# A cosformer attention feeding a leaky-ReLU feed-forward: the first batch's k tails are loaded and prepared first, and its preparation work is dealt out differently between ScalarE and VectorE

## The chip, the cores and the metric

The kernel runs on one core of one Trainium2 chip. The metric is the device time of one execution in microseconds, as the median of several runs. The kernel before takes 294.44 us (three runs, 294.29 to 294.61).

A core has five engines that work through their own instruction queues and meet by semaphores: TensorE (PE in the profile, with its weight loads as PEld), VectorE (DVE), ScalarE (ACT), GpSimd (POOL) and SyncE (SP), which here issues nearly all of the DMA transfers. Main memory is HBM, on-chip memory is SBUF, and the matmul accumulators are in PSUM.

## The reference

Eight batches, eight heads, 576 positions, 64 elements a head. Each of q and k is cut at zero and weighted by the cosine and by the sine of its position, so that a head has 128 features; then a linear attention is formed, and its output is fed to a two-layer network with a leaky ReLU.

```python
def phi(x, c, s):
    r = np.maximum(x, 0.0)
    return np.concatenate([r * c, r * s], axis=-1)
q_p = phi(q, cos_w, sin_w)
k_p = phi(k, cos_w, sin_w)
kv = np.einsum('bhsf,bhsd->bhfd', k_p, v)
z = np.sum(k_p, axis=2)
num = np.einsum('bhsf,bhfd->bhsd', q_p, kv)
den = np.einsum('bhsf,bhf->bhs', q_p, z)[..., None] + 1e-06
attn = num / den
...
x = attn.transpose(0, 2, 1, 3).reshape(B * S, H * D)   # 4608 x 512
h = x @ w_in                                          # 512 x 2048
out = np.maximum(0.01 * h, h) @ w_out                 # 2048 x 512
```

## The kernel before

The 4608 rows go through the network in nine groups of 512: the 512 "main" positions of each of the eight batches, and a ninth group made of the eight 64-position "tails". Weights are cast to float16 once and stay in SBUF. From about 19 us on TensorE runs the two layers back to back, and the attention of the next batch is woven between them. The change lies wholly in what comes before that: the attention of batch 0, which no network work can cover, because the network has nothing to work on yet.

There is no scheduler. The order of the text is the order of every engine's queue, and an engine that waits holds up everything behind it in its own queue.

How batch 0 goes, with the names of the code:

- SyncE issues the loads in the order of the text. `load_main` fetches half of the heads (0 to 3, or 4 to 7) of q, k or v into a staging buffer, 512 KB in rows of 1 KB. `load_kvtail` fetches the 64 tail positions of k or v as two transfers of 64 KB in rows of 256 bytes. Before, the order is q half 0, q half 1, k tail, k half 0, v tail, v half 0, k half 1, v half 1, and then w_in. All of these go through one queue; there are seven staging buffers.
- `idle(n)` issues n matmuls on a tile of zeros, whose result nobody reads. They keep TensorE running while it has nothing to do.
- `q_prep` makes the float16 features of q: for each of two head halves and each j of four position groups one cosine and one sine instruction (`phi_half`, line 226 on VectorE, line 224 on ScalarE). j = 3 is ScalarE's, the others VectorE's.
- `q_transpose` (line 363) turns the features of one j over on TensorE, eight heads, and copies the result from PSUM to SBUF (`qpT`; j = 0, 1, 2 on ScalarE, line 232, j = 3 on VectorE, line 234).
- `k_tail` and `k_main` make the features of k (`kpt` and `kpm`), `v_tail` and `v_main` cast v. Heads 0 to 3 come first. Their features of k are VectorE's, but for the cosine of j = 0, which is ScalarE's; their v is cast half on VectorE and half on ScalarE. For heads 4 to 7 ScalarE has all four cosines and VectorE all four sines.
- `kv_half(0, 0)` sums k features times v over the positions for heads 0 to 3 (lines 264 and 274) into PSUM (`ps_kvh`), and ScalarE copies the sum to `kv` (line 315). `kv_half(0, 1)` does the same for heads 4 to 7.
- `num_half(0, jp, hg)` multiplies q features by `kv` for two of the four j and for four heads (line 409), and `divide` divides by the denominator on VectorE in three instructions (lines 384, 388, 389), giving `xs`.
- `x_transpose_half` (line 425) turns `xs` over on TensorE, and ScalarE copies it to `xT` (line 429), which is what the first layer, `ffn1` (line 452), multiplies.
- GpSimd casts v's tail, the last quarter of v and the pieces of w_in (line 234).

For heads 0 to 3 the order of TensorE's queue after the first `kv_half` is: both `num_half`, six idle matmuls, the turning over of the first two j, `kv_half(0, 1)`, the turning over of the other two j, then the first matmuls of `ffn1` with the same steps for heads 4 to 7 between them.

Two PSUM pools matter here: "o" has two buffers, which idle matmuls, `ps_kvh` and the turned-over `xs` (`ps_xth`) take in turn; "n" has one, and "h" two.

Of the kernel before, what the change touches and what calls it, by code (L numbers as in the profile page):

```python
# [9 lines left out]
dt = mybir.dt  # L10
# [3 lines left out]
P = 128  # L14
J = 4
# [3 lines left out]
def kernel(  # L19
# [14 lines left out]
    nc = tc.nc  # L34
# [11 lines left out]
    NE = D + 2  # L46
# [25 lines left out]
    def psum(where, shape, dtype, name):  # L72
        p = {"h": ps_h, "o": ps_o, "n": ps_n}[where]
        return p.tile(shape, dtype, name=name, tag="ps_" + where)

    st = {}
    ACT, DVE, POOL = nc.scalar, nc.vector, nc.gpsimd
# [3 lines left out]
    def load_main(nm, src, b, parts=(0, 1)):  # L81

        if parts[0] == 0:
            st[nm, b] = stage.tile([P, H, J, D], dt.float32, name=f"{nm}st", tag="stage")
        lo, hi = 4 * parts[0], 4 * parts[-1] + 4
        nc.sync.dma_start(  # L86
            st[nm, b][:, lo:hi],
            src[b, lo:hi, 0:MAIN, :].rearrange("h (p j) d -> p h j d", j=J),
        )

    def load_kvtail(nm, src, b):

        t = kvtail.tile([P, H // 2, D], dt.float32, name=f"{nm}tl", tag="kvtail")
        v4 = src[b, :, MAIN:S, :].rearrange("(c o) p d -> o p c d", o=2)
        for o in range(2):
            nc.sync.dma_start(t[o * TAIL : (o + 1) * TAIL], v4[o])  # L96
        st[nm + "t", b] = t
# [20 lines left out]
    for i in range(DFF // 512):  # L118
        for c in range(0, NKC, 2):
            n = 1 if i == 0 and c == 0 else 2  # L120
# [18 lines left out]
    def load_w2(i, lo=0, hi=4):  # L139
        if lo == 0:  # L140
            st["w2", i] = stage.tile([P, 4, DM], dt.float32, name="w2st", tag="stage")
        nc.sync.dma_start(st["w2", i][:, lo:hi], w2v[i, :, lo:hi])

    load_main("q", q, 0, (0,))
    load_main("q", q, 0, (1,))
    load_kvtail("k", k, 0)
    load_main("k", k, 0, (0,))
    load_kvtail("v", v, 0)
    load_main("v", v, 0, (0,))
# [13 lines left out]
    def idle(n):  # L163
        ps = psum("o", [P, MAIN], dt.float32, "ps_idle")
        for _ in range(n):
            nc.tensor.matmul(ps, lhsT=blank[:, 0:P], rhs=blank)  # L166
# [51 lines left out]
    kv = [const.tile([P, H, NE], dt.float16, name=f"kv{b}") for b in range(B)]  # L218
# [3 lines left out]
    def phi_half(eng, o, i, col):  # L222
        if eng is ACT:
            nc.scalar.activation(o, i, AF.Relu, scale=col)
        else:
            eng.tensor_scalar(  # L226
                out=o, in0=i, scalar1=0.0, scalar2=col, op0=ALU.max, op1=ALU.mult
            )

    def copy(eng, o, i):  # L230
        if eng is ACT:
            nc.scalar.copy(o, i)  # L232
        else:
            eng.tensor_copy(o, i)  # L234

    def kp_tiles(b):
        st["kpm", b] = kppool.tile([P, H, J, F], dt.float16, name="kpm")
        st["kpt", b] = kppool.tile([P, H // 2, F], dt.float16, name="kpt")

    def k_main(b, j, eng_c, eng_s, lo=0, hi=H):  # L240
        kpm, kst = st["kpm", b], st["k", b]
        for eng, t, f in ((eng_c, cos_t, 0), (eng_s, sin_t, D)):
            phi_half(
                eng, kpm[:, lo:hi, j, f : f + D], kst[:, lo:hi, j, :], t[:, j : j + 1]
            )

    def k_tail(b, eng_c, eng_s):
        kpt, kt, c = st["kpt", b], st["kt", b], J
        phi_half(eng_c, kpt[:, :, 0:D], kt, cos_t[:, c : c + 1])
        phi_half(eng_s, kpt[:, :, D:F], kt, sin_t[:, c : c + 1])  # L250

    def v_main(b, lo, hi, eng):
        copy(eng, vmain[b % 2][:, lo:hi, :, 0:D], st["v", b][:, lo:hi])

    def v_tail(b, eng):
        for o in range(2):
            sl = slice(o * TAIL, (o + 1) * TAIL)
            copy(eng, vtail[b % 2][sl, :, o, 0:D], st["vt", b][sl])

    def kv_mm(b, hg, ps):  # L260
        kpm, kpt = st["kpm", b], st["kpt", b]
        for cc in range(2):
            c = 2 * hg + cc
            nc.tensor.matmul(
                ps[:, 2 * cc * NE : 2 * (cc + 1) * NE],
                lhsT=kpt[:, c, :],
                rhs=vtail[b % 2][:, c].rearrange("p a e -> p (a e)"),
                start=True,
                stop=False,
            )  # L270
            for o in range(2):
                h = 2 * c + o
                for j in range(J):
                    nc.tensor.matmul(  # L274
                        ps[:, (2 * cc + o) * NE : (2 * cc + o + 1) * NE],
                        lhsT=kpm[:, h, j, :],
                        rhs=vmain[b % 2][:, h, j, :],
                        start=False,
                        stop=(o == 1 and j == J - 1),
                    )  # L280
# [24 lines left out]
                )  # L305
        nc.scalar.copy(kv[b].rearrange("p (c o) e -> p o c e", o=2), ps)

    def kv_half(b, hg, where, out=True):
        st["kvh", hg] = psum(where, [P, 4 * NE], dt.float32, "ps_kvh")
        kv_mm(b, hg, st["kvh", hg])  # L310
        if out:
            kv_half_out(b, hg)

    def kv_half_out(b, hg):
        nc.scalar.copy(
            kv[b][:, 4 * hg : 4 * hg + 4].rearrange("p h e -> p (h e)"), st["kvh", hg]
        )

    def q_src(g, j):
        if g < B:  # L320
# [3 lines left out]
    def q_prep(g, j, lo=0, hi=H, eng=DVE):  # L324
        src, c, _ = q_src(g, j)
        if lo == 0 and j % 2 == 0:
            st["qp2", g, j // 2] = qppool.tile([P, 2, H, F], dt.float16, name="qp")
            for o in range(2):
                st["qp", g, j + o] = st["qp2", g, j // 2][:, o]
        qp = st["qp", g, j]  # L330
        phi_half(eng, qp[:, lo:hi, 0:D], src[:, lo:hi], cos_t[:, c : c + 1])
        phi_half(eng, qp[:, lo:hi, D:F], src[:, lo:hi], sin_t[:, c : c + 1])
# [26 lines left out]
    def q_transpose(g, j, eng, where="h"):  # L359
        qp = st["qp", g, j]  # L360
        ps = psum(where, [P, H, P], dt.float16, "ps_qt")
        for h in range(H):
            nc.tensor.transpose(ps[:, h, :], qp[:, h, :], ident)  # L363
        if j % 2 == 0:
            qpT_pair(g, j // 2)
        copy(eng, st["qpT", g, j], ps)
# [15 lines left out]
    def divide(ps, xs):  # L382
        den = small.tile([P, H], dt.float32, name="den")
        nc.vector.tensor_scalar_add(  # L384
            den.rearrange("p (a b) -> p a b", a=2), ps[:, :, D : 4 * NE : NE], 1e-6
        )
        rden = small.tile([P, H], dt.float32, name="rden")
        nc.vector.reciprocal(rden, den)  # L388
        nc.vector.tensor_tensor(  # L389
            out=xs,  # L390
            in0=ps[:, :, 0 : 4 * NE].rearrange("p a (b e) -> p a b e", e=NE)[
                :, :, :, 0:D
            ],
            in1=rden.rearrange("p (a b) -> p a b", a=2)[:, :, :, None].broadcast_to(
                [P, 2, 4, D]
            ),
            op=ALU.mult,
        )

    def num_half(g, jp, hg, where, ps=None):  # L400

        if hg == 0 and jp == 0:
            st["xs", g] = xspool.tile([P, J, H, D], dt.float16, name="xs")
        if ps is None:
            ps = psum(where, [P, 2, 512], dt.float32, "ps_numh")
        for o in range(2):
            for hh in range(4):
                h = 4 * hg + hh
                nc.tensor.matmul(  # L409
                    ps[:, o, hh * NE : (hh + 1) * NE],  # L410
                    lhsT=st["qpT", g, 2 * jp + o][:, h, :],
                    rhs=kv[g][:, h, :],
                )
        divide(ps, st["xs", g][:, 2 * jp : 2 * jp + 2, 4 * hg : 4 * hg + 4, :])
# [110 lines left out]

    for hg in range(2):
        for j in range(J):
            q_prep(0, j, 4 * hg, 4 * hg + 4, ACT if j == 3 else DVE)  # L530
    kp_tiles(0)
    q_transpose(0, 0, ACT)
    idle(1)
    q_transpose(0, 1, ACT)
    idle(1)
    k_tail(0, DVE, DVE)
    v_tail(0, POOL)
    k_main(0, 0, ACT, DVE, 0, 4)
    for j in range(1, J):
        k_main(0, j, DVE, DVE, 0, 4)  # L540
    v_main(0, 0, 2, DVE)
    v_main(0, 2, 4, ACT)
    q_transpose(0, 2, ACT, "n")
    idle(1)
    q_transpose(0, 3, DVE)
    idle(7)
    kv_half(0, 0, "o")
    for j in range(J):
        k_main(0, j, ACT, DVE, 4, 8)
    num_half(0, 0, 0, "h")  # L550
    num_half(0, 1, 0, "n")
    v_main(0, 4, 6, ACT)
    v_main(0, 6, 8, POOL)
    idle(6)
    x_transpose_half(0, 0, 0)
    kv_half(0, 1, "o")
    for part in w1_parts:
        cast_w1(*part, POOL)
    x_transpose_half(0, 1, 0)
    half = 2 * P  # L560
    ps = psum("h", [P, 2, 512], dt.float32, "ps_numh")
# [76 lines left out]
    ps = psum("n", [P, 2, DM], dt.float32, "ps_o")  # L638
# [24 lines left out]
    ps = psum("h", [P, 2, MAIN], dt.float16, "ps_x")  # L663
# [124 lines left out]
```

## Time and profile before

| | |
|---|---|
| median of three runs | 294.44 us |
| the profiled execution: time | 293.82 us |
| the profiled execution: span from the first to the last instruction | 292.0 us |
| granted TensorE clock, mean | 1.000 |
| TensorE busy | 286.4 us (98%) |
| VectorE busy | 128.7 us (44%) |
| ScalarE busy | 118.4 us (41%) |
| GpSimd busy | 12.7 us (4%) |
| chain that ended last: TensorE's share | 94% |

The profile's page says "TensorE is the bound" with one look. Idle matmuls count as busy there, though, and 30 of them are 9.9 us. What can be moved at all is the stretch before the network starts, and for that one reads the chain of waits and the order of time of each engine in the first 20 us. Times in those views are from the start of the span; each row gives start, duration, engine, line of the code, operation and tiles, and, in brackets, how long the engine had been idle before it and what ended that.

### The profile page before, as it was taken

What the parts mean: (1) busy time and instruction counts of PE and PEld (TensorE: products, weight loads), DVE (VectorE), ACT (ScalarE), POOL (GpSimd) and SP (SyncE); (2) the same over time, 40 slices, a digit from 0 to 9 for tenths busy, and PEclk for the clock granted to TensorE, in tenths of its full rate; (3) what the DMA queues carried; (4) which work ended last, traced back from release to release, by engine and by line L of the source; (5) the groups of instructions that cost most, each with busy time, mean ns of one, the idle gap of its engine ahead of it and who ended that gap; (6) DMA issues with size and microseconds to landing.
All of it is one profiled execution on the core that took longest, in us unless ns stands there. A gap on an engine that the chain in (4) does not pass through costs nothing.

```text
span 292.0 us, 4774 instructions
## 1 busy us (share of the span) xinstructions
PE 286.4 (98%) x1958; PEld 152.7 (52%) x1958; DVE 128.7 (44%) x328; ACT 118.4 (41%) x148; POOL 12.7 (4%) x24
## 2 busy tenths in 40 slices
PE   8999999999999999999999999999999999999995
PEld 3585556555555555455545554555445444444444
DVE  6931687926835816823562356333323310000011
ACT  6865266753544632632263226322222222222200
POOL 2264000000000000000000000000000000000000
PEclk9999999999999999999999999999999999999999
DMA  7999999999999999789584989504691051011133
GB/s 233 348 386 407 325 364 335 315 204 324 212 241 318 229 291 298 166 162 338 164 182 84 296 233 199 91 37 110 160 199 38 36 108 38 36 54 54 39 71 73
DMA packets 87909, 56.93 MB, mean 195 GB/s; under 512 B 55888, under 2 KB 80720, under 8 KB 87504
## 3 DMA queue, kind: packets, MB, share of 16 engines
q1 hardware_dynamic: 87808, 56.57, 71.0%
q8 instruction: 15, 0.25, 0.4%
q10 hardware_dynamic: 80, 0.07, 0.1%
q14 instruction: 6, 0.05, 0.1%
HBM read 36.70 MB, written 9.44 MB: 158 GB/s over the span
## 4 chain that ended last, share of the span: by engine, by line
PE 94%; DMA 2%; SPq 1%; ACT 1%; DVE 1%; issue 0%
PE ps_h L452 43%; PE ps_o L475 41%; PE ps_num L373 3%; PE ps_kv L299 2%; DMA vst<-in_v_dram 2%; PE ps_l L504 1%; SPq L96 1%; PE ps_xth L425 1%; PE ps_qt L363 1%; PE ps_numh L409 1%; SPq L86 1%; PE ps_kv L290 0%; PE ps_idle L166 0%; PE ps_kvh L274 0%; ACT qpT L232 0%; PE ps_xt L438 0%
## 5 line engine op out<-in xcount | busy, mean ns | idle before, releaser
L452 PE MATMUL ps_h<-xT,w 128*128 128x512 f16 (+1 forms) x592 | 142.8, 373 | 0.1
L475 PE MATMUL ps_o<-w,g 128*128 128x512 f16 x560 | 139.5, 379 | 0.0
L460 ACT ACTIVATE g<-ps_h 128x1024 f16<-128x1024 f32 x72 | 73.2, 1023 | 128.8 <-PE ps_h L452 128.8
L452 PEld LDWEIGHTS <-w 128*128 128x128 f16 x592 | 64.4, 114 | 52.3 <-issue 0.2
L475 PEld LDWEIGHTS <-g 128*128 128x128 f16 x560 | 54.2, 98 | 61.4
L234 DVE COPY osb<-ps_o 128x512 f32<-128x512 f32 x31 | 21.4, 690 | 77.1 <-PE ps_o L475 75.3
L384 DVE TENSOR_SCALAR den<-ps_num 128x8 f32<-128x8 f32 x28 | 4.6, 165 | 54.9 <-PE ps_num L373 54.9
L389 DVE TENSOR_TENSOR xs<-ps_num,rden 128x512 f16<-128x512 f32 x28 | 19.4, 691 | 1.2 <-DVE rden L388 0.2
L226 DVE TENSOR_SCALAR kpm<-kst,sin_t 128x512 f16<-128x512 f32 (+1 forms) x40 | 16.6, 429 | 1.1 <-DMA kst<-in_k_dram 1.1
L226 DVE TENSOR_SCALAR qp<-qst,cos_t 128x512 f16<-128x512 f32 (+1 forms) x34 | 15.5, 456 | 2.8 <-DMA qst<-in_q_dram 2.8
L226 DVE TENSOR_SCALAR qp<-qst,sin_t 128x512 f16<-128x512 f32 (+1 forms) x34 | 15.5, 456 | 0.0
L373 PEld LDWEIGHTS <-qpT 128*128 128x128 f16 (+1 forms) x256 | 10.6, 101 | 7.3 <-issue 1.7
L232 ACT CAST vmain<-vst 128x1024 f16<-128x1024 f32 (+1 forms) x14 | 12.5, 920 | 2.4 <-DMA vst<-in_v_dram 2.3
L226 DVE TENSOR_SCALAR kpm<-kst,cos_t 128x512 f16<-128x512 f32 (+1 forms) x29 | 13.1, 453 | 0.3 <-DMA kst<-in_k_dram 0.3
L373 PE MATMUL ps_num<-kv,qpT 128*128 128x66 f16 (+1 forms) x256 | 11.8, 194 | 0.0
L166 PE MATMUL ps_idle<-blank 128*128 128x512 f16 x30 | 9.9, 478 | 1.2 <-DVE blank L161 1.2
L234 DVE CAST w<-w2st 128x1024 f16<-128x1024 f32 (+1 forms) x6 | 5.1, 868 | 11.8 <-DMA w2st<-in_moe_w_out_dram 11.8
L232 ACT COPY qpT<-ps_qt 128x1024 f16<-128x1024 f16 x7 | 7.0, 1012 | 5.7 <-PE ps_qt L363 5.7
L234 POOL CAST w<-w1st 128x1024 f16<-128x1024 f32 (+1 forms) x9 | 8.5, 945 | 3.6 <-DMA w1st<-in_moe_w_in_dram 3.6
L388 DVE RECIPROCAL rden<-den 128x8 f32<-128x8 f32 x36 | 7.3, 203 | 1.2
L299 PE MATMUL ps_kv<-vmain,kpm 128*128 128x66 f16 x192 | 7.1, 193 | 0.0
L299 PEld LDWEIGHTS <-kpm 128*128 128x128 f16 x192 | 6.4, 98 | 0.3
(62 smaller groups left out, 99.7 us busy)
## 6 DMA issues: line engine op xcount, KB each, us to landing
out_dram<-osb SPq DMA_DIRECT2D x32, 256.0 KB, 2.5
qst<-in_q_dram SPq DMA_DIRECT2D x7, 1024.0 KB, 6.8
kst<-in_k_dram SPq DMA_DIRECT2D x6, 1024.0 KB, 9.7
vst<-in_v_dram SPq DMA_DIRECT2D x6, 1024.0 KB, 9.4
w1st<-in_moe_w_in_dram SPq DMA_DIRECT2D x7, 512.0 KB, 10.4
w2st<-in_moe_w_out_dram SPq DMA_DIRECT2D x3, 1024.0 KB, 12.9
kst<-in_k_dram SPq DMA_DIRECT2D x4, 512.0 KB, 6.9
vst<-in_v_dram SPq DMA_DIRECT2D x4, 512.0 KB, 7.9
```

The costliest lines, as they stand in the source:

```text
L166: nc.tensor.matmul(ps, lhsT=blank[:, 0:P], rhs=blank)
L226: eng.tensor_scalar(out=o, in0=i, scalar1=0.0, scalar2=col, op0=ALU.max, op1=ALU.mult)
L232: nc.scalar.copy(o, i)
L234: eng.tensor_copy(o, i)
L299: nc.tensor.matmul(ps[:, h % 2, h // 2], lhsT=kpm[:, h, j, :], rhs=vmain[b % 2][:, h, j, :], start=False, stop=(h >= H - 2 and j == J - 1),)
L373: nc.tensor.matmul(ps[lo:hi, h // 4, (h % 4) * NE : (h % 4 + 1) * NE], lhsT=qpT[:, h, lo:hi], rhs=kv[b][:, h, :],)
L384: nc.vector.tensor_scalar_add(den.rearrange("p (a b) -> p a b", a=2), ps[:, :, D : 4 * NE : NE], 1e-6)
L388: nc.vector.reciprocal(rden, den)
L389: nc.vector.tensor_tensor(out=xs, in0=ps[:, :, 0 : 4 * NE].rearrange("p a (b e) -> p a b e", e=NE)[:, :, :, 0:D], in1=rden.rearrange("p (a ...
L452: nc.tensor.matmul(ps[:, m % 2, lo:hi], lhsT=w1[m // 4, c][0][:, w1[m // 4, c][1], m % 4 : 512 : 4], rhs=xT[:, lo // P : hi // P, c, :], s ...
L460: nc.scalar.activation(st["g", g][:, m - 1 : m + 1, :], ps, AF.Lrelu)
L475: nc.tensor.matmul(st["ps_o", g, tt], lhsT=st["g", g][:, m, tt * P : (tt + 1) * P], rhs=w2[:, m, :], start=(m == 0), stop=(m == NFT - 1),)
```

## The change

Five edits, all for batch 0:

1. The k tail's two loads go ahead of both halves of q; `k_tail` goes ahead of all of `q_prep` on VectorE.
2. The cosine of j = 1 of k, heads 0 to 3, moves from VectorE to ScalarE.
3. The copy of the first `kv` (heads 0 to 3) moves from ScalarE to VectorE; `kv_half` takes the engine as an argument (and loses an unused option).
4. For heads 4 to 7 the features of k for j = 0 and 1 come first, then the multiplication and division for j = 0 and 1 of heads 0 to 3, then the features for j = 2 and 3, then the second multiplication and division. Before, all four j of k came ahead of both.
5. Three idle matmuls instead of six ahead of the first turning over of `xs`.

```diff
+    load_kvtail("k", k, 0)
     load_main("q", q, 0, (0,))
     load_main("q", q, 0, (1,))
-    load_kvtail("k", k, 0)
     load_main("k", k, 0, (0,))
...
-    def kv_half(b, hg, where, out=True):
-        st["kvh", hg] = psum(where, [P, 4 * NE], dt.float32, "ps_kvh")
-        kv_mm(b, hg, st["kvh", hg])
-        if out:
-            kv_half_out(b, hg)
...
+    def kv_half(b, hg, where, eng=ACT):
+        ps = psum(where, [P, 4 * NE], dt.float32, "ps_kvh")
+        kv_mm(b, hg, ps)
+        copy(eng, kv[b][:, 4 * hg : 4 * hg + 4].rearrange("p h e -> p (h e)"), ps)
...
+    kp_tiles(0)
+    k_tail(0, DVE, DVE)
     for hg in range(2):
         for j in range(J):
             q_prep(0, j, 4 * hg, 4 * hg + 4, ACT if j == 3 else DVE)
-    kp_tiles(0)
     q_transpose(0, 0, ACT)
     idle(1)
     q_transpose(0, 1, ACT)
     idle(1)
-    k_tail(0, DVE, DVE)
     v_tail(0, POOL)
-    k_main(0, 0, ACT, DVE, 0, 4)
-    for j in range(1, J):
-        k_main(0, j, DVE, DVE, 0, 4)
+    for j in range(J):
+        k_main(0, j, ACT if j < 2 else DVE, DVE, 0, 4)
     v_main(0, 0, 2, DVE)
     v_main(0, 2, 4, ACT)
...
-    kv_half(0, 0, "o")
-    for j in range(J):
-        k_main(0, j, ACT, DVE, 4, 8)
-    num_half(0, 0, 0, "h")
-    num_half(0, 1, 0, "n")
+    kv_half(0, 0, "o", DVE)
+    for jp in range(2):
+        for j in range(2 * jp, 2 * jp + 2):
+            k_main(0, j, ACT, DVE, 4, 8)
+        num_half(0, jp, 0, "n" if jp else "h")
     v_main(0, 4, 6, ACT)
     v_main(0, 6, 8, POOL)
-    idle(6)
+    idle(3)
     x_transpose_half(0, 0, 0)
     kv_half(0, 1, "o")
```

More of the change, by code (lines that the diff above doesn't have):

```diff
@@ L306, in kv_all @@
         nc.scalar.copy(kv[b].rearrange("p (c o) e -> p o c e", o=2), ps)
-    def kv_half(b, hg, where, out=True):
-        st["kvh", hg] = psum(where, [P, 4 * NE], dt.float32, "ps_kvh")
-        kv_mm(b, hg, st["kvh", hg])
-        if out:
-            kv_half_out(b, hg)
[L314 to L317, printed above, removed]
+    def kv_half(b, hg, where, eng=ACT):
+        ps = psum(where, [P, 4 * NE], dt.float32, "ps_kvh")
+        kv_mm(b, hg, ps)
+        copy(eng, kv[b][:, 4 * hg : 4 * hg + 4].rearrange("p h e -> p (h e)"), ps)
     def q_src(g, j):
```

## The prediction

> **What bounds the kernel now.** I read the chain of waits first. In time order it shows what held the start up:
>
> ```profile
> 5.19 5.22 DMA vst<-in_v_dram
> 10.43 0.62 ACT vmain L232
> 11.05 0.91 ACT qpT L232
> 11.96 0.29 ACT kv L315
> 12.29 0.67 PE ps_numh L409 x16
> 12.96 1.29 PE ps_idle L166 x6
> 14.61 0.59 ACT xT L429
> 15.24 0.38 PE ps_xth L425 x4
> 18.82 12.11 PE ps_h L452 x64
> ```
>
> From 18.82 us on the chain is TensorE without a hole. Ahead of that it hangs on the landing of v's first half (10.41), then on ScalarE, where the copy of `kv` stands behind a copy of `qpT`. The point to follow is 15.24: the second turning over of `xs` (j = 2, 3). Whatever it shifts by, `ffn1` and all later work of TensorE shift by.
>
> Then the timeline of SyncE's queue, VectorE and ScalarE in the same stretch:
>
> ```profile
> 0.73 1.01 SPq L86 DMA_DIRECT2D qst<-in_q_dram  x2
> 1.79 1.40 SPq L96 DMA_DIRECT2D ktl<-in_k_dram  x2
> 3.23 0.60 SPq L86 DMA_DIRECT2D kst<-in_k_dram  x1
> ...
> 4.65 0.35 DVE L226 TENSOR_SCALAR qp<-qst,cos_t 128x256 f16<-128x256 f32 x1 [1.20 <-DMA qst<-in_q_dram]
> 6.29 0.51 ACT L224 ACTIVATE qp<-qst,cos_t 128x256 f16<-128x256 f32 x1 [0.54 <-DMA qst<-in_q_dram]
> 11.94 1.14 DVE L226 TENSOR_SCALAR kpm<-kst,sin_t 128x256 f16<-128x256 f32 x4 [0.29 <-DMA kst<-in_k_dram]
> 14.46 0.69 DVE L389 TENSOR_TENSOR xs<-ps_numh,rden 128x512 f16<-128x512 f32 x1
> ```
>
> q's halves are waited for at 4.65 and 6.29, k's second half at 11.94. From 11.94 VectorE does four sines and two divisions without a hole until 14.46 + 0.69 = 15.15: 3.21 us. That chain, from a landing, ends 0.09 us ahead of 15.24.
>
> The table of windows shows when the transfers start (the last two columns are the DMA engines' busy share and GB/s):
>
> ```profile
> 1.75:2.00 0.25, 0.25 (x2) 0.00 (x0) 0.25 (x1) 0.25 (x1) 0.25 (x1) 1.00 0.13 37
> 2.75:3.00 0.25, 0.25 (x2) 0.13 (x1) 0.23 (x2) 0.24 (x2) 0.03 (x1) 1.00 1.06 365
> ```
>
> First bytes about 1.1 us after the first issue, then a ramp of 0.9 us to a full share. In windows of 3 us the share stays between 1.01 and 1.21 from 3 to 63 us: the transfers are one saturated stream, so a delay at its head is a delay of every landing up to there.
>
> Last, the next place where TensorE meets a landing, batch 1's first turning over of `xs`:
>
> ```profile
> 44.77 1.14 DVE L226 TENSOR_SCALAR kpm<-kst,sin_t 128x256 f16<-128x256 f32 x4 [0.82 <-DMA kst<-in_k_dram]
> 47.29 0.69 DVE L389 TENSOR_TENSOR xs<-ps_numh,rden 128x512 f16<-128x512 f32 x1
> 48.09 0.61 PE L425 MATMUL ps_x<-ident,xs 128*128 128x128 f16 x8
> ```
>
> `xs` is done at 47.98 from a landing at 44.77, and read at 48.09. So a start that is earlier by more than about 0.1 us is taken back here, unless the stream is earlier too; a later stream has the same 0.1 us.
>
> **The change part by part.**
>
> *The k tail ahead of q in the queue.* Its two issues take 1.40 us from 1.79, so q's first issue moves from 0.73 to about 2.1, by 1.36 (1.40 less the 0.04 between issues that stands there either way). k's half stays at 3.23, and all behind it. How much later q lands is bounded from both sides. Below: from q's second half (6.26) to the v tail (issued 4.53, landing 4.4 later, 8.93) the stream carried two tails and 512 KB; the next 512 KB halves came 1.5 apart (10.41, 11.94), so a 128 KB tail costs (2.67 - 1.53) / 2 = 0.57, about 0.5 with the reading error of the landings. But q's first packet cannot come before its issue: 2.1 + 1.1 = 3.2, where the stream before had already moved 0.32 MB of q by the quarter-microsecond windows. At 380 GB/s, the rate after the ramp, that is 0.85; so q is 0.85 late at the least. Above: the ramp, an engine by engine start, is paid again, and q is late by the whole 1.36. I take 1.15, nearer to the upper end, since the ramp's row is one in which issue and not bandwidth decides. Everything behind q no longer has the tail ahead of it in the stream, which gives 0.5 back: late by 0.65 (ends 0.35 and 0.86).
>
> A rule of the Trainium skill speaks to the size of that 0.5: "DMA: Bandwidth & Descriptors", section "Why small descriptors are slow (HBM only)", charges pieces of 256 bytes 27% on top. By it the tail takes 128 KB / 380 GB/s x 1.27 = 0.44, and the stream would be 0.71 late, not 0.65; the row decides.
>
> *VectorE ahead of `kv`.* The tail's two sines and cosines (2 x 0.265 by their start-to-start) go into the wait for q, and one cosine leaves. They are a new wait at the head of VectorE's queue, with all of `q_prep` behind it; the second tail issue ends near 2.1, 3.7 ahead of q's landing, and the shortest issue to landing at that time is 3.8 for 512 KB, so I count it as covered (a tail that lands after 5.3 would delay q's features one for one). With q at 5.80 and 7.44: six instructions to 7.39, six to 9.03, then six for k (before eight with the tail's) from k's landing 8.43 + 0.65 = 9.08 to 10.67. v lands at 10.41 + 0.65 = 11.06, so VectorE waits for it: cast 11.08 to 11.50, `qpT` of j = 3 (0.68) to 12.15. The 0.8 us taken off VectorE is spent waiting.
>
> *ScalarE ahead of `kv`.* The first copy of `qpT` needs the first j of q's second half, so it moves by 1.15, from 7.39 to 8.54. Two copies take 1.82 (7.39 to 9.21): 10.36. Two cosines instead of one, 0.41 each: 11.18. Before, ScalarE then had 0.71 of idle time until v landed; now the delay and the moved cosine use it up. v's cast goes 11.18 to 11.80 (before 10.43 to 11.05), and behind it `qpT` of j = 2 (0.91). The matmuls of heads 2, 3 need that cast: 11.85 to 12.27 (before 11.41 to 11.83), +0.44.
>
> *The copy of `kv` on VectorE.* No row has it there. Bounds: 0.29, what the chain gives ScalarE for it, and 0.45 (a division's 128x8 costs 0.15, 512 elements out of PSUM 0.69, so 264 come to 0.43). I take 0.40. On ScalarE it would have waited for `qpT` until 12.7, so here the move is right: 12.30 to 12.70, and the multiplication starts at 12.74 (before 12.29). Behind it on VectorE stand the four sines; k's second half lands at 11.94 + 0.65 = 12.59, so they lose 0.11 to the copy.
>
> *The divisions.* Their order changes, not their sum: two sines to 13.23, the division for j = 0, 1 (its matmuls done at 13.08) to 14.3, two sines, the second division. The first `xs` is done at 14.3, not 14.11, and the last at 12.70 + 3.21 = 15.91; the second turning over follows at 15.96 against 15.24: **+0.72**. Even with every landing where it was, this chain could not end before 11.94 + 3.21 = 15.15.
>
> *Heads 4 to 7.* ScalarE is free of `qpT` at 12.62, four cosines (1.61) to 14.23, v (landed 14.1) to 14.83; `kv_half(0, 1)` then runs 14.89 to 15.6, ahead of 15.96. It costs nothing under that cover; without it 0.4 would show.
>
> *Three idle matmuls fewer.* 0.65 us of TensorE that waited for `xs` anyhow: nothing. The PSUM buffer that the second turning over takes is freed by ScalarE's `xT`, 0.94 after the first turning over begins (14.26 to 15.20): 14.35 + 0.94 = 15.3, ahead of 15.96. GpSimd's v cast and the casts of w_in move with the stream, 0.65; w_in's third piece is done at 17.2 and first used at 18.65, so that slack stays.
>
> *At 48 us* the stream is 0.65 late with 0.1 of slack, TensorE 0.72: no further wait.
>
> **The sum:** 293.82 + 0.72 = 294.54 for an execution like the profiled one. That one is 0.62 below the median of the runs, so on the median 295.16; I say **295.15**.
>
> **The rivals.** *No second ramp* (q 0.85 late, stream 0.35). ScalarE: 7.39 + 0.85 + 1.82 + 0.82 = 10.88, v to 11.50, matmuls 11.55 to 11.97, `kv` to 12.4, then 3.21: 15.61, turning over at 15.66, +0.42: **294.85**. For it: the engines are already running when q's issue reaches them; against: each of the 16 DMA engines gets its part of q only after the issue.
>
> *Not slower: the tails travel in the ramp.* If they fill the 0.9 us in which the engines stand half empty, and issue faster as the first in the queue, the stream behind them is earlier by some 0.1: k at 11.84, `kv` already copied, xs at 15.05, -0.1: **294.3**. It decides only if two tails are issued in less than about 0.9 us; the shortest of 32 tail issues took 0.607, so two take 1.2. A larger gain meets the wait at 48 us. Both bounds hold whatever the moved cosine and copy save.
>
> *TensorE's clock falls.* With q late, TensorE turns over heads 0 to 3 of j = 0 by 6.9, and waits till 8.05. The first 512-column matmuls take 427 ns each, later ones 216, so it starts at half speed. If the gap of 1.1 us sends it back until about 13, `kv_half` (0.72 from 11.10 to 11.83) doubles, and the first eight matmuls of the multiplication (0.25) do: some 0.95 on top of the forecast, **296.1**. Against: the gap from 11.83 to 12.29, short as it is, did nothing. "TensorE: Matmul & The Clock Gate" of the Trainium skill, "What's actually happening", has the clock fall after an idle window of about 3.4 us. By it this gap is too short, but part 4 of that page adds that transposes do not count as work; the trace shows no fall either way.
>
> **How the numbers follow.** Forecast 54% (own range 294.95 to 295.4), no second ramp 24%, not slower 12%, clock 10%. The range 294.3 to 295.9 takes in the first three and leaves out the clock and a little on either side. A measurement of this kernel can tell 0.2%, 0.59 us, from no change. Slower by more: the forecast but for its lower part, and the clock, 58%. Within: no second ramp, most of "not slower", that lower part, 37%. Faster 5%.
>
> **What would show it.** Right: q's first wait on VectorE ends near 5.8 and its second at 7.4, k's second half lands near 12.6, the second turning over near 16.0; an idle VectorE ahead of v's cast. Wrong: q's first wait ends before 5.2, or k's second half by 12.0; a `kv` copy over 0.5; 512-column matmuls of 427 ns after 8 us. A new wait of TensorE after 19 us would break the sum too.

## The result, and the profile after

| | before | after |
|---|---|---|
| median | 294.26 us (6 runs, 293.89 to 294.61) | 296.35 us (6 runs, 295.75 to 297.88) |
| ratio, with its 95% interval | | 1.0074 (1.0050 to 1.0098) |
| profiled execution: time, span | 293.82, 292.0 us | 296.38, 294.6 us |

The change costs 2.1 us. It was forecast to cost 0.7, with 295.9 as the far end of the range.

The chain of waits of the kernel after, with start, duration and what ran:

```profile
2.21 4.59 DMA qst<-in_q_dram
6.82 2.20 DVE qp L226 x8
9.07 0.40 PE ps_qt L357 x4
...
11.46 1.51 PE ps_idle L166 x7
...
13.63 0.43 DVE kv L234
14.06 0.53 DVE kpm L226 x2
...
15.00 0.69 DVE xs L383
15.69 0.99 DVE kpm L226 x2
...
17.03 0.70 DVE xs L383
17.78 0.40 PE ps_xth L419 x4
...
21.37 12.11 PE ps_h L446 x64
```

The chain no longer begins with v's landing but with q's. From there it goes through the features of q, their turning over, `kv`, then sines and divisions in turn, to the second turning over of `xs`. That one stood at 15.24 and is now at 17.78: +2.54, and the span is longer by 2.6. Two equal sounding rows differ: the sines at 14.06 took 0.53 for two, those at 15.69 took 0.99.

The timeline of the kernel after, in brackets the idle time before the row and what ended it:

```profile
0.73 1.44 SPq L96 DMA_DIRECT2D ktl<-in_k_dram  x2
2.21 1.16 SPq L86 DMA_DIRECT2D qst<-in_q_dram  x2
...
6.82 0.35 DVE L226 TENSOR_SCALAR qp<-qst,cos_t 128x256 f16<-128x256 f32 x1 [2.13 <-DMA qst<-in_q_dram]
8.21 0.51 ACT L224 ACTIVATE qp<-qst,cos_t 128x256 f16<-128x256 f32 x1 [0.42 <-DMA qst<-in_q_dram]
12.21 0.43 DVE L234 CAST vmain<-vst 128x512 f16<-128x512 f32 x1
15.31 0.61 POOL L234 CAST vmain<-vst 128x512 f16<-128x512 f32 x1 [3.81 <-DMA vst<-in_v_dram]
15.61 1.08 DVE L226 TENSOR_SCALAR kpm<-kst,sin_t 128x256 f16<-128x256 f32 x2
```

q is issued 1.48 later (0.73 to 2.21) but waited for until 6.82 and 8.21, 2.17 and 1.92 later than before. The last quarter of v, for which GpSimd waits, lands 1.79 later (13.52 to 15.31). The late sines of VectorE, at 15.61, run while GpSimd casts.

The windows of the kernel after (busy time of PE, PEld, DVE, ACT, POOL, then granted clock, DMA share and GB/s), and below them the first five microseconds of the kernel before:

```profile
0.00:5.00 5.00, 3.81 (x10) 1.42 (x11) 2.92 (x13) 3.26 (x5) 2.05 (x11) 1.00 0.33 93
2.75:3.00 0.25, 0.25 (x2) 0.13 (x1) 0.22 (x3) 0.24 (x2) 0.03 (x1) 1.00 0.18 40
3.75:4.00 0.25, 0.25 (x2) 0.13 (x1) 0.00 (x0) 0.25 (x1) 0.00 (x0) 1.00 0.30 66
4.50:4.75 0.25, 0.25 (x2) 0.14 (x1) 0.19 (x1) 0.24 (x1) 0.00 (x0) 1.00 1.20 356
```

```profile
0.00:5.00 5.00, 3.81 (x9) 1.34 (x10) 2.66 (x13) 3.31 (x6) 2.05 (x11) 1.00 0.58 201
```

Before, the DMA engines reached their full rate at 2.75; now at 4.50, 1.75 later. In five microseconds they moved 93 GB/s x 5 us = 0.47 MB instead of 1.00. The missing 0.53 MB are 1.4 us at 370 to 380 GB/s. By 10 us the gap is still 0.49 MB (207 against 256 GB/s): hardly anything has been made good.

At the second place that the forecast watched, around 48 us of the kernel after:

```profile
46.38 1.14 DVE L226 TENSOR_SCALAR kpm<-kst,sin_t 128x256 f16<-128x256 f32 x4 [0.82 <-DMA kst<-in_k_dram]
...
48.90 0.69 DVE L383 TENSOR_TENSOR xs<-ps_numh,rden 128x512 f16<-128x512 f32 x1
...
50.65 0.61 PE L419 MATMUL ps_x<-ident,xs 128*128 128x128 f16 x8
```

The landing is 1.61 later, the turning over 2.56. `xs` is ready 1.06 ahead of its reader, where it had 0.1 to spare. No new wait arose; the loss comes whole from the first 18 us.

### The profile page after: what moved, and what is told of

It reads as the page before. It is cut to its first block, busy times and chain, and to the rows that moved or that the text cites. A ratio compares the mean times of both kernels' runs of the same rounds, so it can differ in the third digit from the quotient of the medians.

```text
span 294.6 us, 4766 instructions
## 1 busy us (share of the span) xinstructions
PE 285.4 (97%) x1955; PEld 152.1 (52%) x1955; DVE 129.3 (44%) x328; ACT 118.6 (40%) x148; POOL 12.6 (4%) x24
## 4 chain that ended last, share of the span: by engine, by line
PE 94%; DVE 3%; DMA 2%; SPq 0%; issue 0%; ACT 0%
PE ps_h L446 42%; PE ps_o L469 41%; PE ps_num L367 3%; PE ps_kv L299 2%; DMA qst<-in_q_dram 2%; PE ps_qt L357 1%; PE ps_l L498 1%; DVE qp L226 1%; PE ps_idle L166 1%; DVE xs L383 1%; PE ps_xth L419 1%; PE ps_kvh L274 1%; DVE kpm L226 1%; SPq L96 0%; PE ps_kv L290 0%; PE ps_numh L403 0%
## 5 line engine op out<-in xcount | busy, mean ns | idle before, releaser
L166 PE MATMUL ps_idle<-blank 128*128 128x512 f16 x27 | 8.5, 455 | 1.2 <-DVE blank L161 1.2
L357 PE MATMUL ps_qt<-ident,qp 128*128 128x128 f16 x64 | 5.1, 219 | 2.6 <-DVE qp L226 2.6
```

## The experiments

Ratios are to the kernel before, measured in the same series. "q's waits end" gives the times at which an engine stops waiting for q's first and second half, "turning over" that of the second one of `xs`, both in the profiled execution.

| run | median us | ratio (95%) | q's waits end | turning over |
|---|---|---|---|---|
| before_again | 294.24 | 0.9996 (0.9980 to 1.0011) | 4.64, 6.43 | 15.53 |
| e6_edits1and4_undone | 294.19 | 0.9996 (0.9984 to 1.0008) | 4.65, 6.22 | 16.34 |
| e1_edit1_undone | 294.75 | 1.0011 (0.9998 to 1.0024) | 4.64, 6.34 | 16.17 |
| e8_half_tail_first | 295.89 | 1.0047 (1.0028 to 1.0065) | 6.28, 7.91 | 16.87 |
| e4_tail_second | 296.20 | 1.0074 (1.0047 to 1.0101) | 4.83, 7.75 | 17.35 |
| e2_load_order_only | 296.27 | 1.0074 (1.0046 to 1.0103) | 6.37, 7.70 | 16.79 |
| e7_khalf_first | 296.40 | 1.0070 (1.0056 to 1.0083) | 6.22, 8.69 | 17.90 |
| e11_fewer_idle | 296.53 | 1.0075 (1.0055 to 1.0094) | 6.93, 8.33 | 17.72 |
| e9_waits_filled | 296.80 | 1.0075 (1.0058 to 1.0091) | 6.96, 8.37 | 18.61 |
| e5_edit4_undone | 297.60 | 1.0105 (1.0065 to 1.0145) | 7.02, 8.45 | 19.92 |
| e10_tail_loads_doubled | 298.26 | 1.0125 (1.0095 to 1.0155) | 4.60, 6.16 | 17.83 |
| e3_tail_on_act_queue | 299.58 | 1.0187 (1.0165 to 1.0210) | no wait, 7.07 | 20.83 |

**The kernel before, once more** (unchanged). One execution had been the base of every difference.

> The kernel before, profiled a second time, since its first profiled execution was 0.6 us under the median of its runs. If the landings vary from one execution to the next, v's first half or k's second half lands 0.2 us or more off 10.4 and 11.9, and the second turning over of xs is off 15.24 by as much; otherwise every row repeats to 0.05 us.

Its profiled execution took 294.36 us with a span of 292.6. q's second half was waited for until 6.43, v until 10.70, k's second half until 12.21; the turning over stood at 15.53. So these landings differ by 0.14 to 0.27 between two executions of one kernel, the turning over by 0.29, and the first profile was an early one. Against this one the change moves the turning over by 2.25 and the span by 2.0, which is what the medians say.

**Edit 1 taken back, edits 2 to 5 kept.**

```diff
 (after)
-    load_kvtail("k", k, 0)
     load_main("q", q, 0, (0,))
     load_main("q", q, 0, (1,))
+    load_kvtail("k", k, 0)
...
-    k_tail(0, DVE, DVE)
     for hg in range(2):
...
     idle(1)
+    k_tail(0, DVE, DVE)
     v_tail(0, POOL)
```

> Load order and place of the k tail's features as before; edits 2 to 5 stay. Theory H (head of the stream): nearly all of the 2.1 us comes from the two tail loads at the head of the queue, so q's first wait on VectorE ends at 4.65 again and the second turning over of xs comes back from 17.78 to 15.3 to 16.0. Inside H, if the two sines that ran at 0.54 instead of 0.265 us did so because GpSimd worked beside them, they still do here, and 0.4 to 0.7 us over before are left; if not, 0 to 0.2. Rival W (the work dealt out): the moved copy, cosine and division cost by themselves, 1.2 us or more over before are left.

294.75 us, 1.0011: of the 0.74% only 0.11% is left, 0.3 us, between the two expectations, and the interval takes in no difference at all. The turning over, at 16.17, is a little later than the 15.3 to 16.0 expected. Its timeline:

```profile
13.71 0.61 POOL L234 CAST vmain<-vst 128x512 f16<-128x512 f32 x1 [3.78 <-DMA vst<-in_v_dram]
13.83 1.25 DVE L226 TENSOR_SCALAR kpm<-kst,sin_t 128x256 f16<-128x256 f32 x2
...
16.17 0.40 PE L419 MATMUL ps_xth<-ident,xs 128*128 128x128 f16 x4 [0.39 <-DVE xs L383]
```

The loss belongs to edit 1. But what is left is no gain either: two sines that GpSimd's casts run beside took 1.25, where two alone take 0.61 (12.19 of the same execution).

**The load order alone, in the kernel before.**

```diff
 (before)
+    load_kvtail("k", k, 0)
     load_main("q", q, 0, (0,))
     load_main("q", q, 0, (1,))
-    load_kvtail("k", k, 0)
```

> The kernel before with one edit, the k tail's loads ahead of q's; all preparation as before. H: q lands near 6.8 as in the changed kernel, ratio to before 1.006 to 1.007 (1.7 to 2.0 us). W: under 1.0 us.

296.27 us: one line moved gives the whole loss. The timeline:

```profile
6.37 0.35 DVE L226 TENSOR_SCALAR qp<-qst,cos_t 128x256 f16<-128x256 f32 x1 [2.91 <-DMA qst<-in_q_dram]
7.70 0.51 ACT L224 ACTIVATE qp<-qst,cos_t 128x256 f16<-128x256 f32 x1 [0.46 <-DMA qst<-in_q_dram]
11.97 0.62 ACT L232 CAST vmain<-vst 128x512 f16<-128x512 f32 x1 [0.59 <-DMA vst<-in_v_dram]
13.48 1.14 DVE L226 TENSOR_SCALAR kpm<-kst,sin_t 128x256 f16<-128x256 f32 x4 [0.25 <-DMA kst<-in_k_dram]
```

Here v's and k's landings are seen as waits: 1.27 later than in the second profile of before, for both. With e1 it settles which edit it was.

**The tail through ScalarE's queue.** If SyncE's issue time is the cost, another queue should spare it.

```diff
 (after)
-    def load_kvtail(nm, src, b):
+    def load_kvtail(nm, src, b, queue=nc.sync):
...
-            nc.sync.dma_start(t[o * TAIL : (o + 1) * TAIL], v4[o])
+            queue.dma_start(t[o * TAIL : (o + 1) * TAIL], v4[o])
...
-    load_kvtail("k", k, 0)
+    load_kvtail("k", k, 0, nc.scalar)
```

> The changed kernel, but ScalarE issues the k tail's two loads, so SyncE's first issue is q at 0.73. H by the issue: q lands within 0.5 us of 4.65 and the time is that of e1 within 0.3 us. H by the small rows (the 256-byte rows at the head hold the DMA engines up, whoever issues them): q lands 1.2 us or more late, time at least 1.0 us over e1.

299.58 us: the time says nothing on the issue, for this became another experiment. Its timeline:

```profile
7.43 0.35 DVE L226 TENSOR_SCALAR kpt<-ktl,cos_t 128x256 f16<-128x256 f32 x1 [3.98 <-DMA ktl<-in_k_dram]
...
7.96 0.35 DVE L226 TENSOR_SCALAR qp<-qst,cos_t 128x256 f16<-128x256 f32 x1
```

q's first half was there by 5.43, when ScalarE used it. VectorE had the tail's features first in its queue, and the tail landed at 7.43. All of q stood behind it, TensorE waited 2.87 us and then 1.18, and from 10.70 to 14.10 its granted clock was 0.52. The stream itself does answer the question: q's first half landed 4.2 us after its issue, at 4.9, within the 0.5 us of 4.65 that was expected if the issue is the cost, and by 5 us 0.88 MB had been moved (175 GB/s), against 1.00 before and 0.47 in the kernel after, with the same tail loads on the way. What starves the stream is that q stands behind the tail in one queue.

**The tail between the halves of q.** `k_tail` goes between the halves of `q_prep` too.

```diff
 (after)
-    load_kvtail("k", k, 0)
     load_main("q", q, 0, (0,))
+    load_kvtail("k", k, 0)
     load_main("q", q, 0, (1,))
```

> Loads in the order q half 0, k tail, q half 1; the tail's features between the two halves of q; edits 2 to 5 stay. H: the stream has q's first 512 KB to work on while the tails are issued, so q's first half lands at 4.65, and the time is e1 plus at most 0.4 us. Rival (issue time costs wherever it stands): q's second half lands 1.4 late, near 7.7, and the time is e1 plus 0.8 or more.

296.20 us. q's first half came as in before (4.83), the second 1.3 to 1.5 later (7.75): an issue of two tails costs this much behind a half of q as well, though 512 KB were already under way. The load order theory, as it stood, had called this place nearly free and was wrong; the price goes with the issue time.

**Edit 4 taken back: all four sines ahead of both divisions.**

```diff
 (after)
-    for jp in range(2):
-        for j in range(2 * jp, 2 * jp + 2):
-            k_main(0, j, ACT, DVE, 4, 8)
-        num_half(0, jp, 0, "n" if jp else "h")
+    for j in range(J):
+        k_main(0, j, ACT, DVE, 4, 8)
+    num_half(0, 0, 0, "h")
+    num_half(0, 1, 0, "n")
```

> The changed kernel with all four sines of heads 4 to 7 ahead of both divisions again. Theory C (contention): the two late sines took 0.54 instead of 0.265 each because GpSimd's casts ran beside them; ahead of the divisions they run from 14.06 to 15.1, before GpSimd starts at 15.3, take 1.06 for four, and the second turning over of xs comes 0.4 to 0.5 us earlier, at 17.3. Rival N: the order is neutral (the sum is the same), 17.8 stays, or it is later because the first division waits.

Four runs from 295.56 to 298.73: nothing on the sines. But windows of its profiled execution (298.49) show something else, in the column of the granted clock:

```profile
9.50:10.07 0.57, 0.57 (x12) 0.45 (x9) 0.57 (x3) 0.36 (x1) 0.00 (x0) 0.99 1.12 265
10.07:13.48 3.41, 3.41 (x25) 2.49 (x23) 3.08 (x9) 3.41 (x6) 0.79 (x2) 0.50 1.10 343
13.48:14.00 0.52, 0.52 (x3) 0.20 (x2) 0.27 (x1) 0.52 (x2) 0.00 (x0) 1.00 1.10 353
```

For 3.41 us TensorE had half its clock. Eight turnings over took 1.06 instead of 0.61, the `kv` copy came at 15.48 instead of 13.63. All four sines then ran while GpSimd cast, and took 1.92.

**Edits 1 and 4 both taken back**, so that 2, 3 and 5 are left: the two diffs of e1 and e5 together.

> Only edits 2, 3 and 5 stay (second cosine on ScalarE, kv copied by VectorE, three idle matmuls). C: four sines at 0.265, second turning over at 15.2 to 15.4, 0.8 earlier than the 16.17 of the kernel with edits 2 to 5, time as before within 0.1%. N: it stays at 16.0 to 16.2.

294.19 us, 0.9996: these three edits neither gain nor lose what can be measured. Its timeline:

```profile
13.05 1.13 DVE L226 TENSOR_SCALAR kpm<-kst,sin_t 128x256 f16<-128x256 f32 x4
...
14.55 0.61 POOL L234 CAST vmain<-vst 128x512 f16<-128x512 f32 x1 [4.84 <-DMA vst<-in_v_dram]
```

Four sines end ahead of GpSimd's start and take 1.13, less than e1's last two. From the end of the `kv` copy to the end of the last `xs` are 3.12 us here (13.13 to 16.25) and 3.85 in e1 (12.27 to 16.12), a stretch that does not depend on when v landed: edit 4 cost 0.73 there. The medians of e1 and e6 are 0.56 apart, 0.44 by their ratios, but the intervals overlap: the rows show the slowing, its price in the whole time is not settled to a tenth. (v landed late in this execution, at 11.45, 1.02 later than in the first profile of before, with the same load order; that is why the turning over is at 16.34 and not at the 15.2 to 15.4 expected. It took 294.91, above its median.)

**A half of k ahead of q instead of the tail**: four times the bytes, a third of the issue time.

```diff
 (before)
+    load_main("k", k, 0, (0,))
     load_main("q", q, 0, (0,))
     load_main("q", q, 0, (1,))
     load_kvtail("k", k, 0)
-    load_main("k", k, 0, (0,))
```

> The kernel before with k's first half (512 KB, rows of 1 KB, one issue) ahead of q in place of the tail. Theory S (a stream that is fed too slowly while it is empty): this issue feeds 512 KB in 0.5 us, so nothing is lost from the stream: q's first half is 1.4 late by its bytes (near 6.0), but v's first half lands at 10.4 and k's second at 11.9 as before; time +0.4 to +0.8 us. Rival O (whatever stands ahead of q costs alike): v's first half lands 1.2 or more late as with the tails, time +1.5 us or more.

296.40 us. The stream is not behind: 1.63 MB by 7 us, before 1.60. So the issue time is what starves the stream, as expected. The time is lost all the same: q's halves are 1.6 and 2.3 to 2.4 late (6.22, 8.69), since now 512 KB stand ahead of them, and the turning over is at 17.90. That is 2.0 us more than before, where the expectation from the issue time had 0.4 to 0.8 and left v and k's second half where they were; they landed 0.4 to 0.7 late. 512 KB are 1.4 us at 380 GB/s, so q's second half lost 0.9 to 1.0 more: from 7.0 to 8.5 us, with the four tail loads on their way, the DMA engines were busy (a share of 1.30) but moved 218 GB/s, before 269 to 290. Whatever goes ahead of q costs, one way by issue time, the other by bytes.

**Only one of the two tail loads ahead of q.**

```diff
 (before)
+    load_kvtail("k", k, 0, (0,))
     load_main("q", q, 0, (0,))
     load_main("q", q, 0, (1,))
-    load_kvtail("k", k, 0)
+    load_kvtail("k", k, 0, (1,))
```

> The kernel before with one of the k tail's two loads ahead of q, the other behind it. S, in proportion to the issue time: q's first half lands 0.8 to 1.0 late (5.4 to 5.7), v's first half 0.6 to 0.9 late (11.0 to 11.3), time +0.7 to +1.1 us. Rival (one cold start, paid once whatever its size): q 1.6 or more late, time +1.6 us or more.

295.89 us, 1.5 more than before: between the two expectations. By 5 us 0.66 MB were moved, 0.34 behind, for 0.8 us of issue. A part goes with the issue time; q's first half, 1.6 late, paid most of its price with the first tail already, as the rival of one cold start had it.

**TensorE's waits filled with idle matmuls**, to keep the clock up.

```diff
 (after)
-    idle(14)
+    idle(20)
...
         for h in range(H):
+            if g == 0 and j == 0 and h == 4:
+                idle(5)
             nc.tensor.transpose(ps[:, h, :], qp[:, h, :], ident)
```

> The changed kernel with idle matmuls in TensorE's two waits for q (six more ahead of the first turning over, five between its heads 3 and 4). Theory K (the clock gate): the executions near 298 us are those in which the clock fell to half for 3.4 us after these waits; with the waits filled none is over 297.0 and the median is 295.8 to 296.3. Rival: they come from late landings; then about one in six is still over 297.

296.80 us, no better, and above the 295.8 to 296.3 expected; two runs, 297.05 and 297.20, are over the 297.0 that none should have passed. All six runs have a mean granted clock of 1.000, while 8 of the 29 runs of the kernels with tail loads ahead of a half of q in SyncE's queue (after, e2, e4, e5, e8, e11) have 0.993 or 0.994. At that rate six clean runs come about one time in seven by chance, so this is a hint. And the filling got into the way: the first copy of `qpT` came at 10.18 instead of 9.51, 0.67 later, where q was 0.14 later.

**The tail loaded twice, behind q.** The first copy goes to a spare buffer that nobody reads.

```diff
 (before)
     load_main("q", q, 0, (1,))
+    spare = kvtail.tile([P, H // 2, D], dt.float32, name="spare", tag="kvtail")
+    for o in range(2):
+        nc.sync.dma_start(
+            spare[o * TAIL : (o + 1) * TAIL],
+            k[0, :, MAIN:S, :].rearrange("(c o) p d -> o p c d", o=2)[o],
+        )
     load_kvtail("k", k, 0)
```

> The kernel before with the k tail loaded twice, one copy unused, both behind q, where the stream is full. If a tail costs its bytes there (0.5 us of the stream, as the forecast took it): q lands as before, v's first half 0.4 to 0.6 late, time +0.2 to +0.6 us. If it costs its issue time there too (1.4 us): v's first half 1.2 or more late, time +1.0 us or more.

The traced execution is its fastest, 296.56 us; the others took 298.14 to 299.44, with mean clocks of 0.987 to 0.994. Its timeline:

```profile
4.60 0.35 DVE L232 TENSOR_SCALAR qp<-qst,cos_t 128x256 f16<-128x256 f32 x1 [1.15 <-DMA qst<-in_q_dram]
9.36 0.35 DVE L232 TENSOR_SCALAR kpm<-kst,sin_t 128x256 f16<-128x256 f32 x1 [0.99 <-DMA kst<-in_k_dram]
12.82 0.62 ACT L238 CAST vmain<-vst 128x512 f16<-128x512 f32 x1 [2.95 <-DMA vst<-in_v_dram]
```

q is on time, v lands 2.1 to 2.4 late, as expected for a price by issue time (1.2 or more). The forecast's price for one more tail in the stream was 0.5, worked out from bytes and landings. The two issues take 1.42, and the issues behind them move by 1.33. Why the landing is later still by 0.8 to 1.1 is open. An empty queue is hardly the reason: from 5 to 10 us the DMA engines were busy (a share of 1.05, before 1.14) but moved 269 GB/s, against 291 to 311 in the two profiles of before, e1 and e6, and only 159 from 6.0 to 6.5 at a share of 0.99.

**Fewer idle matmuls ahead of the first `kv_half`.** In the chain of after seven stand at 11.46.

```diff
 (after)
-    idle(7)
+    idle(3)
     kv_half(0, 0, "o", DVE)
```

> The changed kernel with three idle matmuls instead of seven ahead of the first kv_half. The chain of the changed kernel passes through those seven (1.51 us). If they hold the end: kv_half starts at v's casts, 12.65 to 12.85, instead of 12.97, and the time falls by 0.1 to 0.3 us. If v's cast is just behind them: no change within 0.1 us.

296.53 us, no change. The first `kv_half` begins 0.20 earlier (12.86 to 12.66) and `kv` is copied 0.21 earlier, but the late sines then take 1.22 and the turning over is at 17.72, 0.06 earlier. Time that is won here is given back beside GpSimd.

## Why the prediction was wrong

It had the direction and the way the delay travels, mis-sized two terms and left out a third; the first is the largest. From 15.96 to 17.78 are 1.82, of which 1.36 lie ahead of the end of the `kv` copy (12.70 forecast, 14.06 measured) and 0.46 behind it. With q late by the measured 2.17 the forecast's own chain ends the copy at 13.72, so q's lateness is 1.02 of the 1.36; the other 0.34 are TensorE's, below.

**The step that failed: the k tail ahead of q in the queue.** It had q late by 1.15, between 0.85 and 1.36, and the stream behind it by 0.65, between 0.35 and 0.86, because "a 128 KB tail costs" 0.57 of the stream and "gives 0.5 back". Measured: q late by 1.7 to 2.4 in the profiled executions of after, e2, e5, e9 and e11 for its first half, and the stream by 1.3 to 1.9 (the last quarter of v, against the two profiles of before).

- The upper end, 1.36, took q's issue time for the whole delay. It is no bound: the issue moved by 1.48, the landing by 2.17, and with one tail (e8) by 0.8 and 1.6.
- The 0.5 was not given back. Nothing moves until 2.25, and from there to 4.00 the DMA engines run at 40 to 126 GB/s in two bursts; the full rate comes 1.75 later. The tails' own 0.13 MB are 0.35 us of that at full rate; the other 1.4 us are lost to all that follows. At the head of the queue the price of a tail is for the most part the issue time in which nothing else is queued, not its bytes: q's issue alone moved by 1.48 of the 1.75, and e3 and e7, where SyncE issues 512 KB at once, have 0.88 and 0.97 MB by 5 us, the kernel after 0.47.
- The 27% that the Trainium skill ("DMA: Bandwidth & Descriptors", "Why small descriptors are slow (HBM only)") adds for small pieces does not make up for it: an estimate by that is 0.44 for a tail, and e10's second tail made v 2.1 to 2.4 late.

**ScalarE ahead of `kv`: the mechanism holds.** Its first copy of `qpT` came at 9.51 instead of 7.39, late by 2.12, which is q's first half (2.17) passed on through VectorE's eight feature instructions; two copies and two cosines follow without a hole to v's cast at 12.21. The 0.71 of slack went, as forecast. The idle VectorE ahead of v's cast did not come: by then VectorE was as late as v.

**TensorE ahead of `kv`: a term left out.** The forecast had the matmuls of heads 0 and 1 done when ScalarE's cast of v ended, with 0.42 us to go. But VectorE's cast came as late as ScalarE's, and the seven idle matmuls ran until 12.97; all of `kv_half`, 0.63 us, stood behind them. That is the 0.34, and e11, with four idle matmuls fewer, won 0.21 of it.

**The copy of `kv` on VectorE: right.** 0.43, forecast 0.40.

**The divisions: called neutral, in fact +0.46.** Forecast 3.21 from the end of the copy to the last `xs`, measured 14.06 to 17.73, 3.67. The number of instructions is the same; but the new order puts two sines behind the first division, where GpSimd's casts have begun, and there they took 0.99 in the chain instead of 0.53. In e6, with the old order, the same stretch is 3.12. The trace of before had the warning: a sine and a cosine took 0.48 and 0.53 while GpSimd cast v's tail, their neighbours 0.34 and 0.35.

```profile
8.73 0.35 DVE L226 TENSOR_SCALAR kpm<-kst,cos_t 128x256 f16<-128x256 f32 x1
8.84 0.94 POOL L234 CAST vtail<-vtl 64x256 f16<-64x256 f32 x2 [6.06 <-DMA vtl<-in_v_dram]
8.99 0.48 DVE L226 TENSOR_SCALAR kpm<-kst,sin_t 128x256 f16<-128x256 f32 x1
9.39 0.53 DVE L226 TENSOR_SCALAR kpm<-kst,cos_t 128x256 f16<-128x256 f32 x1
9.85 0.34 DVE L226 TENSOR_SCALAR kpm<-kst,sin_t 128x256 f16<-128x256 f32 x1
```

**At 48 us no further wait, and heads 4 to 7 and the idle matmuls free: right.** That edits 2, 3 and 5 cannot pay was right too (e6).

**The rivals.** "No second ramp" and "the tails travel in the ramp" erred to the other side. "TensorE's clock falls" did not happen in the profiled execution of after, but one of its six runs, 297.88, has a mean clock of 0.994, and e5's trace shows the fall at this place. A mean of 0.994 over 294 us is 1.8 us of clock, as 3.41 us at half clock are 1.7. The rival was right in kind and happens in a part of the runs; the median is not its work, for the five runs of after with a mean clock of 0.999 or 1.000 took 295.75 to 296.44.

**Still open:** why q in after and e8 and v in e10 land 0.7 to 1.1 later than the issue time accounts for; and the price of the sines beside GpSimd, which a run that moves only GpSimd's casts would give and which wasn't tried.

## What to carry to other kernels

When the DMA queues are empty, order the first loads by what their issue holds up: two loads of 64 KB took 1.4 us to issue and starved the stream, one of 512 KB took 0.5; and put nothing ahead of the load that heads the chain. An edit that only reorders an engine's work still needs a look at who else is running at the new time. Profile the kernel before twice: here its own executions differ by 0.3 us at the points from which differences of 0.7 were forecast, and v landed 1.0 us later in one execution with the same load order (e6).

## What the runs showed of the hardware

- **TensorE's clock can fall after short waits.** In e5 it waited 0.63 and 1.18 us for q with turnings over between, then had half its clock for 3.41 us. In the 3.41 us ahead of the fall it was busy for 1.60, of which 0.78 idle matmuls; in after, with waits of 1.42 and 1.18, it was busy for 1.40 and 0.48 in the same stretch, and the clock stayed. In e3, with waits of 2.87 and 1.18, the traced run's clock fell too, and all four runs have a mean of 0.988 to 0.994. The Trainium skill ("TensorE: Matmul & The Clock Gate", "What's actually happening") has a free-running window of about 3.4 us: the length agrees with e5's 3.41, and a window that runs free would explain why only some executions fall. Its fall after an idle window does not fit as it stands, TensorE not having been idle that long, unless, as its part 4 says, transposes don't count as work.
- **VectorE beside GpSimd.** A sine of 128x256, 0.265 from start to start alone, took about 0.5 to 0.6 beside GpSimd's casts (after, e1, e9, e11). The division did not change: 0.69 beside a cast (before, 14.46) and with GpSimd idle (before, 17.63). The casts took 0.61 with or without it, but 0.78 once (e7, at 14.20).
- **First bytes** came some 0.7 to 0.8 us after the end of the first issue and not a fixed time after its start: at 1.85 behind q's issue of 0.46, at about 2.3 behind a tail's of 0.75.
